# Two chained MLPs after attention on one core: the last layer in seven block products from a DRAM scratch, Softplus as one instruction, phases by an integer

## The chip, the core and the metric

The kernel runs on one core of a Trainium2 chip. TensorE (PE) multiplies matrices, VectorE (DVE) and ScalarE (ACT) do the work by element, GpSimd (POOL) next to nothing, SyncE (SP) issues the DMAs. The metric is the device time of one execution in microseconds; three runs of the kernel before had a median of 847.79 (846.71 to 847.88).

## The reference

```python
# attention: 4 x 8 heads, 576 tokens, 64 wide: a band of 7 neighbours, and softmax over 144 pooled tokens
out_up    = np.repeat(sm_attn(q_d, k_d, v_d), 4, axis=2)
out_local = softmax(where(|i - j| < 4, q k^T / 8, -1e9)) @ v
x = (out_up + out_local)  ->  2304 x 512
# first MLP: 512 -> 2048 -> 512
h = x @ w_in;  g = np.maximum(h, 0.0) + np.log1p(np.exp(-np.abs(h)));  x = g @ w_out
# second MLP: 512 -> 2048 -> 512, weights of its own
h = x @ w_in;  g = h * np.cos(h);  return (g @ w_out).astype(np.float32)
```

The MLP weights come as 64-bit floats, which the kernel decodes to 32 bits with shifts and ors.

## The kernel before

Each large product is three fp16 matmuls: operands are scaled and cut into a high and a low half, and hi x hi, hi x lo and lo x hi are added up in PSUM. Tokens are worked in five tiles (0 to 3 of 512 rows, 4 of 256; `TILES`), the 2048 hidden units in 16 units of 128.

Attention and the first MLP overlap. In the first MLP, for every tile and unit, `unit_in` (L1341) multiplies 12 matmuls into PSUM tile `h`; ScalarE makes |h|, relu(h), exp(-|h|) and ln(1 + ...) of it (L1438, L1442, L1446, L1450), VectorE adds them with the scale (L491, called by `mix`), `gh` (L501 on ScalarE or L503 on VectorE) makes the high half and `gl` (L483) the low half; the output layer follows at L1522. Meanwhile the second MLP's weights are loaded and decoded in `Weight.decode` (L636 a ScalarE rebase, L480 and L644 VectorE shift and or, L666 a bound for the scale), `split` makes their halves, and they stay in SBUF, in the space of the first MLP's weights as it comes free.

The input layer of the second MLP is already in seven block products instead of eight (`pair_in`): a pair of units is 7 products of 6 matmuls of 256 columns (L1376), with 14 fp16 blocks of 128 x 256 of weights (halves of 7 combinations), one kept product (`keep`, L1404) and four block sums on VectorE (L483, tile `hs`). Tile 4 takes the plain form (`last_in`). Then `rest_in` works out the activation: ScalarE h/2pi + 1/4 (`turns`, L1463), VectorE rounds it by adding and taking off a large constant (L1468) and subtracts (`rest`, L483 to `ta`), ScalarE takes the sine (L1474), VectorE multiplies with h (`G`, L1478), then `gh` and `gl`. The output layer `l4` (L1572) is the plain product, 512 columns a matmul, with both weight halves in SBUF; its scaled results (L495, L497) are stored by 18 DMAs. Before each tile, `y_in` prepares the input (sums, halves, a maximum for the scale).

The order of the instructions is not that of the code. Every operation is handed to a planner with its engines, a cost, its reads and writes and the buffers it claims; the planner orders each engine's queue by costs and due times, shifted by a table of numbers by operation (`MOVES`), and the order is then fixed. An engine takes its queue in order.

Of the kernel before, what the change touches and what calls it, by code (L numbers as in the profile page):

```python
# [15 lines left out]
I32 = mybir.dt.int32  # L16
I64 = mybir.dt.int64
# [9 lines left out]
NB = NF // 2  # L27
# [6 lines left out]
TWOPI = float(np.float32(2.0 * np.pi))  # L34
INV2PI = float(np.float32(1.0 / (2.0 * np.pi)))
T23 = float(1 << 23)
BELOW = 12
# [20 lines left out]
NST2, NTC, NOS, NHS, NPU = 2, 2, 4, 2, 4  # L58
# [6 lines left out]
W2STEP = 3  # L65
# [97 lines left out]
class Op:  # L163
    def __init__(self, n, cost, fn, claim, name):
        self.n, self.cost, self.fn, self.claim, self.name = n, cost, fn, claim, name
        self.succ, self.wait, self.values = set(), 0, set()
        self.hook, self.key = None, ""
# [238 lines left out]
def build(tc, qk, vw, vd, mask, w1i, w1o, w2i, w2o, out):  # L406
# [3 lines left out]
    with ExitStack() as ctx:  # L410
# [1143 lines left out]
        def l4(t, f):  # L1554
# [3 lines left out]
            if apart:  # L1558
                nd = 2
# [375 lines left out]
```

## Time and profile before

| | |
|---|---|
| median of 3 runs | 847.79 us |
| profiled execution, span | 847.6 us |
| TensorE busy | 834.0 us (98%) |
| VectorE busy | 719.1 us (85%) |
| ScalarE busy | 533.6 us (63%) |
| moved by DMA | 59.57 MB |

An execution is one span from the first instruction to the last. Busy time of an engine is the time in which at least one of its instructions was in work, so an instruction that starts before the one ahead of it has ended counts only for what it adds. Because of this overlap, the distance between two starts in a packed stretch is shorter than the duration listed. The chain of waits follows the work that ended last back to the start. Line numbers are those of the kernel before.

### The profile page before, as it was taken

Reading aid. Unit: us, or ns where it says so; the run is one execution under the profiler, and the core shown is the slowest. Engines: PE = TensorE matmul, PEld = TensorE weight load, DVE = VectorE, ACT = ScalarE, POOL = GpSimd, SP = SyncE. Lnnn points to the kernel's source line nnn. Section 1 sums busy time; section 2 is a strip of 40 time slices with the busy share of each in tenths; the row PEclk is TensorE's granted clock in tenths of the full one; section 3 lists DMA queues with packets and bytes.
Section 4 is the critical chain, followed back from the end, with each engine's and each line's share of the span. In section 5 each row is a group of like instructions: output and inputs, shape, how many; then the busy total and the mean of one; then the engine's idle time right before and its main releaser. Section 6 shows DMA issues by size and latency. Waiting matters only on the chain.

```text
span 847.6 us, 15741 instructions
## 1 busy us (share of the span) xinstructions
PE 834.0 (98%) x6325; PEld 493.8 (58%) x6325; DVE 719.1 (85%) x1482; ACT 533.6 (63%) x964; POOL 1.8 (0%) x9
## 2 busy tenths in 40 slices
PE   8988999999999999999999999999999999999998
PEld 4634545455545555444467886676666565676664
DVE  7989999997767858999968999998779679889763
ACT  5478996686635747699977876556444335555441
POOL 0000000000000000000000000000000000000000
PEclk9999999999999999999999999999999999999999
DMA  9876441112110300342023200000000100100010
GB/s 321 281 277 240 162 173 41 51 33 64 61 45 1 117 1 2 120 178 100 1 99 107 94 2 1 1 1 29 23 1 1 51 1 1 51 1 2 2 50 25
DMA packets 14361, 59.57 MB, mean 70 GB/s; under 512 B 1681, under 2 KB 1809, under 8 KB 10193
## 3 DMA queue, kind: packets, MB, share of 16 engines
q1 hardware_dynamic: 14288, 58.58, 19.9%
q8 instruction: 49, 0.80, 0.4%
q14 instruction: 24, 0.19, 0.1%
HBM read 53.85 MB, written 4.72 MB: 69 GB/s over the span
## 4 chain that ended last, share of the span: by engine, by line
PE 89%; ACT 5%; DVE 3%; DMA 2%; issue 0%; POOL 0%; POOLq 0%; ACTq 0%; SPq 0%
PE any L1572 22%; PE h L1376 20%; PE any L1522 19%; PE h L1341 19%; PE any L1314 1%; PE any L1097 1%; PE any L1850 1%; DMA stg<-w1o 1%; PE any L817 1%; PE any L972 1%; PE h L1277 1%; DMA stg<-w1i 1%; ACT w1i_t L636 1%; ACT w1i_t L495 0%; DVE w1i_t L644 0%; ACT ed L937 0%
## 5 line engine op out<-in xcount | busy, mean ns | idle before, releaser
L1572 PE MATMUL any<-w1i_t,g 128*128 128x512 f16 x864 | 197.8, 379 | 0.5 <-DVE w1o_t L497 0.5
L1341 PE MATMUL h<-xt,w1i_t 128*128 128x512 f16 (+1 forms) x888 | 179.5, 356 | 0.1
L1376 PEld LDWEIGHTS <-w2i_t 128*128 128x128 f16 x1536 | 150.2, 98 | 31.6 <-issue 0.3
L1522 PE MATMUL any<-g,w1o_t 128*128 128x512 f16 (+1 forms) x792 | 157.2, 353 | 0.0
L1572 PEld LDWEIGHTS <-g 128*128 128x128 f16 x864 | 84.5, 98 | 88.4 <-issue 1.1
L1341 PEld LDWEIGHTS <-w1i_t 128*128 128x128 f16 x888 | 86.1, 98 | 83.0 <-issue 2.6
L1522 PEld LDWEIGHTS <-w1o_t 128*128 128x128 f16 x888 | 85.7, 98 | 79.9 <-issue 1.4
L483 DVE TENSOR_TENSOR g<-td,g 128x512 f16<-128x512 f32 (+1 forms) x146 | 92.0, 630 | 8.9 <-ACT g L501 6.0
L1376 PE MATMUL h<-xt,w2i_t 128*128 128x256 f16 x720 | 94.3, 273 | 0.1
L1474 ACT ACTIVATE tc<-ta 128x512 f32<-128x512 f32 (+1 forms) x80 | 46.8, 585 | 66.7 <-DVE ta L483 64.6
L1376 PE MATMUL h<-w1o_t,w2i_t 128*128 128x256 f16 x624 | 78.9, 273 | 0.0
L501 ACT ACTIVATE g<-td 128x512 f16<-128x512 f32 (+1 forms) x81 | 48.4, 598 | 38.8 <-DVE td L1478 28.1
L1463 ACT ACTIVATE ta<-hs,quarter,i 128x512 f32<-128x512 f32 x64 | 51.5, 808 | 30.2 <-DVE hs L483 29.6
L1438 ACT ACTIVATE ta<-h,i 128x512 f32<-128x512 f32 (+1 forms) x74 | 47.1, 637 | 25.7 <-PE h L1341 21.4
L1478 DVE SCALAR_TENSOR_TENSOR td<-hs,r,tc 128x512 f32<-128x512 f32 x64 | 48.0, 750 | 13.7 <-ACT tc L1474 12.5
L483 DVE TENSOR_TENSOR hs<-h,hs 128x512 f32<-128x512 f32 (+1 forms) x96 | 57.2, 598 | 2.4 <-PE h L1376 1.6
L483 DVE TENSOR_TENSOR ta<-ta,tb 128x512 f32<-128x512 f32 (+1 forms) x80 | 50.9, 636 | 1.4
L1442 ACT ACTIVATE tb<-h,r 128x512 f32<-128x512 f32 (+1 forms) x74 | 47.1, 636 | 5.9 <-PE h L1341 4.0
L1450 ACT ACTIVATE ta<-ta,one 128x512 f32<-128x512 f32 (+1 forms) x74 | 49.8, 675 | 1.4
L491 DVE SCALAR_TENSOR_TENSOR td<-ta,sg,tb 128x512 f32<-128x512 f32 (+1 forms) x64 | 43.6, 682 | 7.8 <-ACT ta L1450 6.8
L1468 DVE TENSOR_SCALAR tb<-ta 128x512 f32<-128x512 f32 (+1 forms) x80 | 31.8, 398 | 17.1 <-ACT ta L1463 16.3
L1446 ACT ACTIVATE ta<-ta 128x512 f32<-128x512 f32 (+1 forms) x74 | 43.1, 585 | 0.3
(198 smaller groups left out, 1045.1 us busy)
## 6 DMA issues: line engine op xcount, KB each, us to landing
qk<-qk SPq DMA_DIRECT2D x16, 589.0 KB, 5.9
stg<-w1i SPq DMA_DIRECT2D x8, 1024.0 KB, 6.0
stg<-w1o SPq DMA_DIRECT2D x8, 1024.0 KB, 5.0
stg<-w2i SPq DMA_DIRECT2D x8, 1024.0 KB, 4.9
stg<-w2o SPq DMA_DIRECT2D x8, 1024.0 KB, 4.7
vw<-vw SPq DMA_DIRECT2D x16, 320.0 KB, 5.5
out<-w1o_t SPq DMA_DIRECT2D x18, 256.0 KB, 2.0
vd<-vd SPq DMA_DIRECT2D x8, 288.0 KB
```

Of the source, the lines that this page charges most:

```text
L483: eng[e].tensor_tensor(out=out, in0=in0, in1=in1, op=op)
L501: nc.scalar.activation(out=out, in_=in_, func=AF.Copy)
L1341: nc.tensor.matmul(h.t[:, 0:n], l, r, start=(i == 0), stop=(i == 11))
L1376: nc.tensor.matmul(h.t[:, a : a + 256], l, r, start=(i == 0), stop=(i == n - 1))
L1438: act(n, 1, True), lambda: nc.scalar.activation(out=a(), in_=h.t[:, 0:n], func=AF.Abs, scale=col(o.i1, f)),
L1442: act(n, 1, True), lambda: nc.scalar.activation(out=b(), in_=h.t[:, 0:n], func=AF.Relu, scale=col(o.r1, f)),
L1450: act(n, 1), lambda: nc.scalar.activation(out=a(), in_=a(), func=AF.Ln, bias=one),
L1463: act(n, 2, psum), lambda: nc.scalar.activation(out=a(), in_=h.t[:, a0 : a0 + n], func=AF.Identity, scale=col(o.i2, f), bias=quarter), [h, ...
L1474: act(n), lambda: nc.scalar.activation(out=r(), in_=a(), func=AF.Sin, scale=TWOPI),
L1478: dve(n, False, 1), lambda: nc.vector.scalar_tensor_tensor(out=td.t[:, 0:n], in0=h.t[:, a0 : a0 + n], scalar=col(o.r1, f), in1=r(), op0=AL ...
L1522: nc.tensor.matmul(a.t[:, i, 0:n], l, r, start=(first and j == 0), stop=(last and j == 2))
L1572: nc.tensor.matmul(a.t[:, i], l, r, start=(f == 0 and j == 0), stop=(f == NF - 1 and j == 2))
```

## The change

1. **Output layer of the second MLP** in seven block products: 256-column matmuls, 336 a tile (168 in tile 4) in place of 192 (96) of 512 columns. Its left operands are seven blocks of g for a pair of units, four of them sums made on VectorE (`S`), and all seven get a high and a low half. Seven VectorE instructions a tile join the products to the result, and the results are stored in pieces of 256 columns.
2. **DRAM scratch.** The decoded and split matrices of the second MLP are written to DRAM (`scr_in`, `scr_out`) and streamed back for every tile: for a pair of units 917 KB into one of two buffers (`RI`), for an output product two halves of 524 KB into two of four (`RO`). Decoding has a second ScalarE pass (`top`) and one VectorE instruction fewer. All these loads are in SP's queue.
3. **Softplus.** In tiles 1 to 4 of the first MLP a single ScalarE instruction takes the place of |h|, relu, exp, ln and VectorE's sum; attention pairs from the eighth on take their exponentials as Softplus of a value lowered by 20. Functions of different tables now follow each other on ScalarE: 48 table loads in the program instead of 2.
4. **Phases.** `turns` writes an integer; one VectorE instruction multiplies h again and takes that integer off; the rounding instruction goes, and the quarter turn is given to the sine.
5. Tile 2 of the second MLP's input layer takes the plain form (512 columns). Tile 0's input layer runs among tile 4 of the first MLP. From tile 2 on, ScalarE makes a sum of magnitudes (`xsum`) where VectorE made a maximum. The table `MOVES` is new throughout.

```diff
-NST2, NTC, NOS, NHS, NPU = 2, 2, 4, 2, 4
+NST2, NDEC, NRI, NRO, NTC, NHS, NPU, NGF = 2, 4, 2, 4, 3, 2, 3, 2
+ONES, FROM, LONG = range(0, 10, 2), (4, 0), (2, 4)
 MOVES = {
-    "L1 0 0": -32.5, "L1 0 10 exp#1": 38.5, "L1 0 10 gl#1": 66, "L1 0 10 mm#1": 57, "L1 0 11 abs#1": 73,
+    "L1 0 0": -800, "L1 0 1": 102, "L1 0 1 mm#1": -108, "L1 0 10 relu#1": 41.5, "L1 0 11": 13, "L1 0 12 mm#1": -24.5,
...
+        def block_in(t, b):
+            w = RI.new()
+            P.add(
+                dma(917), lambda: nc.sync.dma_start(w.t, scr_in[b]), [("scr", "w2i", b), "place3"], [w], [w], f"L3 {t} {2 * b} load"
+            )
+            return w
...
+        def turn_in(t, f, h, keys, g, psum, a0=0, hold=()):
...
+                    out=bits(a()), in_=x(), func=AF.Identity, scale=col(o.i2, f), bias=quarter
...
+                    out=a(), in0=x(), scalar=col(o.i2, f), in1=bits(a()), op0=ALU.mult, op1=ALU.subtract
...
+                act(n, 1), lambda: nc.scalar.activation(out=r(), in_=a(), func=AF.Sin, scale=TWOPI, bias=halfpi),
...
+        def parts_in(t, b, g):
...
+            for o, a, c, op in ((1, 7, 4, ALU.add), (2, 1, 0, ALU.subtract), (3, 0, 7, ALU.subtract), (5, 6, 2, ALU.subtract)):
+                P.add(dve(n), lambda o=o, a=a, c=c, op=op: two("dve", at(o), at(a), at(c), op), [], [g], name=nm + "S")
...
+            for v, a, m in ((u[0][0], 0, 1), (u[1][0], 1, 2), (u[3][0], 3, 2), (u[5][0], 5, 2)):
...
+                P.add(dve(n * m), lambda x=x, hi=hi, lo=lo: two("dve", lo(), x(), hi(), ALU.subtract), [g], [v], [], nm + "gl")
...
+            if t:
+                v = (TA, TB)[f % 2].new()
+                x = lambda: v.t[:, 0:n]
+                P.add(
+                    act(n, 1, True), lambda: nc.scalar.activation(out=x(), in_=h.t[:, 0:n], func=AF.Softplus, scale=col(o.i1, f)),
+                    [h, *sc], [v], [v], nm + "soft", table="sp",
+                )
...
+            then = [
+                (0, 0, 0, lambda: p.update(p1=take(0))), (1, 2, 5, lambda: p.update(u2=join(1, p["p1"], OS_.new()))),
+                (2, 1, 4, lambda: None), (3, 3, 1, seventh),
+                (0, 4, 6, lambda: out_rows(join(0, p["u3"], p["u3"]), 1, 0)),
+                (1, 5, 3, lambda: out_rows(join(1, p["u4"], p["u4"]), 0, 1)),
+                (2, 6, 2, lambda: out_rows(join(2, p["p1"], p["p1"]), 0, 0)),
+            ]
+            for j, (k, s, pos, fn) in enumerate(then):
+                ws = []
+                for h in range(2):
+                    w = RO.new()
+                    ws.append(w)
+                    P.add(
+                        dma(524), lambda w=w, pos=pos, h=h: nc.sync.dma_start(w.t, scr_out[:, pos, 4 * h : 4 * h + 4]),
+                        [("scr", "w2o", b) for b in range(NB)] + ["place3"], [w], [w], f"L4 {t} {j} load",
+                    )
+                for c in range(m):
+                    for b in range(NB):
...
+                            for x, (l, r) in enumerate(((gh, wh), (gh, wl), (gl, wh))):
+                                nc.tensor.matmul(
+                                    a.t[:, z, 256 * c : 256 * c + 256], l, r, start=(b == 0 and x == 0),
+                                    stop=(b == NB - 1 and x == 2),
+                                )
...
+                def store():
+                    if self.name == "w2i":
+                        nc.sync.dma_start(scr_in[b], both())
+                    else:
+                        for h in range(2):
+                            nc.sync.dma_start(scr_out[:, :, b, h], both()[:, h].rearrange("p (k e) -> p k e", k=7))
```

How the order of VectorE's queue reads in the second MLP, while pairs of tile 0 are in work, before (`hs` are the joined sums of h, `ta` and `tb` the turns and their rounded form, `tc` the sine, `td` the product, `g` halves, `xt` the next tile's input):

```order
L1468 TENSOR_SCALAR tb_97<-ta_94 128x512
L491 SCALAR_TENSOR_TENSOR xt_81<-xt_81,sx_199,xs_99 128x512
L483 TENSOR_TENSOR ta_94<-ta_94,tb_97 128x512
L483 TENSOR_TENSOR hs_4944<-h_757,pu_4947 128x512
L1250 COPY xt_81<-xs_99 128x512
L1478 SCALAR_TENSOR_TENSOR td_98<-hs_4943,r_0_169,tc_4941 128x512
L1234 TENSOR_REDUCE xm_212<-xt_82 128x1
L483 TENSOR_TENSOR hs_4943<-h_756,hs_4943 128x256
L483 TENSOR_TENSOR g_102<-td_98,g_102 128x512
L491 SCALAR_TENSOR_TENSOR xt_81<-xt_81,sx_199,xs_99 128x512
L1468 TENSOR_SCALAR tb_96<-ta_95 128x512
```

And after, with pairs of tile 1 in work (`gf` holds the eight blocks of g of a pair; the low halves go into the space of the first MLP's weights, `w1i_t` and `w1o_t`):

```order
L1509 SCALAR_TENSOR_TENSOR ta_98<-hs_4429,i_1_180,ta_98 128x512
L513 TENSOR_TENSOR hs_4430<-h_3135,hs_4430 128x512
L513 TENSOR_TENSOR gf_4434<-gf_4434 128x256
L513 TENSOR_TENSOR hs_4430<-h_3134,hs_4430 128x256
L513 TENSOR_TENSOR gf_4434<-gf_4434 128x256
L1509 SCALAR_TENSOR_TENSOR ta_97<-hs_4430,i_1_180,ta_97 128x512
L533 CAST w1o_t<-gf_4434 128x512
L1518 SCALAR_TENSOR_TENSOR gf_4435<-hs_4429,r_1_183,tc_4428 128x2x256
L513 TENSOR_TENSOR w1i_t<-gf_4434,w1i_t 128x256
L513 TENSOR_TENSOR w1o_t<-gf_4434,w1o_t 128x512 x2
L1509 SCALAR_TENSOR_TENSOR ta_98<-hs_4430,i_1_180,ta_98 128x512
L513 TENSOR_TENSOR w1i_t<-gf_4434,w1i_t 128x512
```

The rounding (L1468) is gone; the remainder (L1509) has become a three-operand instruction. Sums within `gf` stand between the input layer's sums, and four low halves a pair stand where two stood, three of them as wide as before.

ScalarE's queue in the first MLP, where the second MLP's weights are decoded, before (`w2i_t` is a weight block, `h` a unit's product):

```order
L495 ACTIVATE w2i_t<-w2i_t,s_w2i 128x1792
L1450 ACTIVATE ta_95<-ta_95,one 128x512
L495 ACTIVATE tx_3405<-tx_3405,sx_175 128x512
L1438 ACTIVATE ta_94<-h_757,i_3_201 128x512
L501 ACTIVATE g_103<-td_98 128x512
L1446 ACTIVATE ta_94<-ta_94 128x512
L1442 ACTIVATE tb_96<-h_756,r_3_205 128x512
L1450 ACTIVATE ta_94<-ta_94,one 128x512
L501 ACTIVATE g_105<-td_98 128x512
```

And after (`stg` is a block as loaded, `dec` the decoded one, L1869 the rebase, L1874 the added pass, L1887 the bound, L1553 Softplus):

```order
L525 ACTIVATE g_110<-tb_99,sg_194 128x512
L1869 ACT_TABLE_LOAD
L1869 ACTIVATE dec_3168<-stg_3166 128x1024
L1874 ACTIVATE stg_3166<-stg_3166,nearhalf 128x1024
L1869 ACTIVATE dec_3169<-stg_3167 128x1024
L1553 ACT_TABLE_LOAD
L1553 ACTIVATE ta_97<-h_781,i_2_191 128x512
L1887 ACT_TABLE_LOAD
L1887 ACTIVATE stg_3166,bd_w2i<-dec_3168 128x1024
L1874 ACTIVATE stg_3167<-stg_3167,nearhalf 128x1024
L1887 ACTIVATE stg_3167,bd_w2i<-dec_3169 128x1024
L1553 ACT_TABLE_LOAD
```

Four functions a unit have become one, and each change between Softplus and the decode's functions has a table load ahead of it.

## Rows read from the trace of the kernel before

**Rows 1.** The page's busy times: us, share of the span, instructions

```profile
PE 834.0 (98%) x6325; PEld 493.8 (58%) x6325; DVE 719.1 (85%) x1482; ACT 533.6 (63%) x964; POOL 1.8 (0%) x9
```

**Rows 2.** The page's chain of waits, by engine and by line

```profile
PE 89%; ACT 5%; DVE 3%; DMA 2%; issue 0%; POOL 0%; POOLq 0%; ACTq 0%; SPq 0%
PE any L1572 22%; PE h L1376 20%; PE any L1522 19%; PE h L1341 19%; PE any L1314 1%; PE any L1097 1%; PE any L1850 1%; DMA stg<-w1o 1%; PE any L817 1%; PE any L972 1%; PE h L1277 1%; DMA stg<-w1i 1%; ACT w1i_t L636 1%; ACT w1i_t L495 0%; DVE w1i_t L644 0%; ACT ed L937 0%
```

**Rows 3.** Busy times by stretch (us; instructions; granted clock; DMA share; GB/s)

```profile
150.00:300.00 150.00, 150.00 (x1317) 77.59 (x1315) 123.38 (x280) 98.62 (x197) 0.00 (x0) 1.00 0.15 50
300.00:430.00 130.00, 129.99 (x791) 64.27 (x789) 117.50 (x249) 101.96 (x164) 0.00 (x0) 1.00 0.19 65
...
600.00:700.00 100.00, 99.73 (x651) 63.42 (x649) 75.34 (x128) 39.72 (x63) 0.00 (x0) 1.00 0.03 11
...
520.00:560.00 40.00, 40.00 (x270) 26.11 (x267) 40.00 (x84) 22.97 (x37) 0.00 (x0) 1.00 0.00 1
```

**Rows 4.** Pieces of the chain: start us, length us, what

```profile
488.28 9.84 PE h L1376 x90
...
829.45 14.26 PE any L1572 x66
...
843.73 0.69 ACT w1o_t L495
```

**Rows 5.** Groups of TensorE by line and form: busy us, mean ns

```profile
L1572 PE MATMUL any<-w1i_t,g 128*128 128x512 f16 x864 | 197.8, 379 | 0.5 <-DVE w1o_t L497 0.5
...
L1376 PEld LDWEIGHTS <-w2i_t 128*128 128x128 f16 x1536 | 150.2, 98 | 31.6 <-issue 0.3
```

**Rows 6.** Timeline of VectorE in the second MLP: start us, length us

```profile
531.96 0.75 DVE L1478 SCALAR_TENSOR_TENSOR td<-hs,r,tc 128x512 f32<-128x512 f32 x1
532.62 0.42 DVE L1234 TENSOR_REDUCE xm<-xt 128x1 bf16<-128x256 f32 x1
532.95 0.42 DVE L483 TENSOR_TENSOR hs<-h,hs 128x256 f32<-128x256 f32 x1
533.28 0.42 DVE L1468 TENSOR_SCALAR tb<-ta 128x512 f32<-128x512 f32 x1
533.61 0.69 DVE L483 TENSOR_TENSOR g<-td,g 128x512 f16<-128x512 f32 x1
534.21 0.69 DVE L483 TENSOR_TENSOR ta<-ta,tb 128x512 f32<-128x512 f32 x1
```

**Rows 7.** Groups of VectorE by line and form: busy us, mean ns

```profile
L1478 DVE SCALAR_TENSOR_TENSOR td<-hs,r,tc 128x512 f32<-128x512 f32 x64 | 48.0, 750 | 13.7 <-ACT tc L1474 12.5
...
L644 DVE SCALAR_TENSOR_TENSOR w2i_t<-stg,w2i_t 128x1024 int32<-128x1024 int32 x8 | 9.8, 1223 | 0.0
```

**Rows 8.** Groups of ScalarE by line and form: busy us, mean ns

```profile
L1450 ACT ACTIVATE ta<-ta,one 128x512 f32<-128x512 f32 x58 | 41.7, 721 | 1.0
...
L1438 ACT ACTIVATE ta<-h,i 128x512 f32<-128x512 f32 x58 | 39.7, 684 | 25.1 <-PE h L1341 21.4 <-DVE td L491 2.7 <-DVE am L1217 0.7
L1442 ACT ACTIVATE tb<-h,r 128x512 f32<-128x512 f32 x58 | 39.6, 683 | 4.0 <-PE h L1341 4.0
L1446 ACT ACTIVATE ta<-ta 128x512 f32<-128x512 f32 x58 | 36.5, 631 | 0.1
...
L636 ACT ACTIVATE w2i_t<-stg 128x1024 f32<-128x1024 f32 x8 | 9.2, 1149 | 1.2 <-DMA stg<-w2i 1.2
```

**Rows 9.** Timeline of ScalarE around its second table load

```profile
495.16 0.81 ACT L1463 ACTIVATE ta<-hs,quarter,i 128x512 f32<-128x512 f32 x1 [0.57 <-DVE hs L483]
495.99 1.28 ACT L1474 ACT_TABLE_LOAD   x1
```

**Rows 10.** The page's GB/s by slice, and DMA issues (KB each, us to landing)

```profile
GB/s 321 281 277 240 162 173 41 51 33 64 61 45 1 117 1 2 120 178 100 1 99 107 94 2 1 1 1 29 23 1 1 51 1 1 51 1 2 2 50 25
...
stg<-w2i SPq DMA_DIRECT2D x8, 1024.0 KB, 4.9
...
out<-w1o_t SPq DMA_DIRECT2D x18, 256.0 KB, 2.0
```

More of the change, by code (lines that the diff above doesn't have):

```diff
@@ L180, in __init__, with add @@
         self.ops, self.wrote, self.read, self.time = [], {}, {}, {}
-    def add(self, cost, fn, reads=(), writes=(), claim=(), name="", after=()):
-        op = Op(len(self.ops), cost, fn, claim, name)
+    def add(self, cost, fn, reads=(), writes=(), claim=(), name="", after=(), table=""):
+        op = Op(len(self.ops), cost, fn, claim, name, table)
         pre = set(after)
@@ L329, in order @@
                     end = now + op.cost[e]
+                    if e == "act" and loaded not in SETS[op.table]:
+                        end, loaded = end + LOAD, SETS[op.table][0]
                     free[e] = end
@@ L726, in build, with aop @@
         stages = {}
-        def aop(cost, fn, reads=(), writes=(), claim=(), name=""):
+        def aop(cost, fn, reads=(), writes=(), claim=(), name="", table=""):
             stage = name.split()[-1]
-            op = P.add(cost, fn, reads, writes, claim, name, stages.get(stage, ()) if claim else ())
+            op = P.add(cost, fn, reads, writes, claim, name, stages.get(stage, ()) if claim else (), table)
             if claim:
@@ L937, in B2 @@
                     nc.scalar.activation(
-                        out=row(t), in_=src, func=AF.Exp, scale=float(2.0**-7),
+                        out=row(t), in_=src, func=power, scale=float(2.0**-7),
                         bias=nd.t[:, t : t + 1], accum_out=r.t[:, 2 * NG + t : 2 * NG + t + 1],
@@ L1237, in max_x, with sum_x, total @@
             )
+        def sum_x(t, c):
+            v = TC_.new()
+            def total():
+                with nc.allow_low_precision(reason="a bound, for the choice of a scale"):
+                    nc.scalar.activation(
+                        out=v.t[:, 0 : TILES[t][1]], in_=xt[t][:, c, :], func=AF.Abs, accum_out=col(T[t].xm, c)
+                    )
+            P.add(act(TILES[t][1], 1), total, [xkey(t, c), "place3"], [("xm", t, c), v], [v], name="xsum", table="pr")
         def split_x(t, c):
@@ new lines, in turn_in @@
+            P.add(
+                act(n, 1), lambda: nc.scalar.activation(out=r(), in_=a(), func=AF.Sin, scale=TWOPI, bias=halfpi),
+                [ta, "place3"], [tr], [tr], nm + "sin", table="tr",
+            )
+            P.add(
+                dve(n, False, 1), lambda: nc.vector.scalar_tensor_tensor(
+                    out=at(), in0=two_of(x()), scalar=col(o.r1, f), in1=two_of(r()), op0=ALU.mult, op1=ALU.mult
+                ), [*keys, tr, *sc], [g], [g, *hold], nm + "G",
+            )
@@ new lines, in join, with seventh @@
+            def join(k, x, o):
+                P.add(
+                    dve(256 * m, False, 1), lambda: nc.vector.scalar_tensor_tensor(
+                        out=o.t[:, 0 : 256 * m], in0=view(k), scalar=T[t].ik, in1=x.t[:, 0 : 256 * m],
+                        op0=ALU.mult, op1=ALU.add,
+                    ), [(t, k), x, ("sc", t)], [o], [o, acc[k][0]], "osb",
+                )
+                return o
+            p = {}
+            def seventh():
+                p["u4"] = p["u2"]
+                p["u3"] = join(3, p["u2"], OS_.new())
+                join(2, p["u2"], p["u2"])
+                out_rows(join(2, p["u3"], OS_.new()), 1, 1)
@@ L1700, in tx_part @@
+        W2I, W2O = Second("w2i", w2i), Second("w2o", w2o)
+        txs = [TX.new() for _ in range(5)]
         def tx_part(t, u, n=1):
-            return (txs[t].t if t else tx0[0])[:, 512 * u : 512 * (u + n)]
+            return txs[t].t[:, 512 * u : 512 * (u + n)]
         def tx_float(t, k):
@@ L1741, in y_in @@
             for c in range(NC_):
-                if c < 2 and t < 4:
+                if c < 2 and t not in LONG:
                     split_half(t, c)
@@ L1813, in build @@
+        drain(0)
         for p in sorted(pos):
             assert p < at, (p, at)
[L1815 to L1834 removed]
@@ L1835, in build @@
-        drain(0)
+        mms = {W: [o for o in P.ops if o.name[:3] == k and "pe" in o.cost] for W, k in ((W1I, "L1 "), (W1O, "L2 "))}
+        for W, ops in mms.items():
+            for u in range(NF + 1):
+                bs = [b for b in range(NB) if u in (W.hunit(b), W.funit(b))]
+                names = [f"{t} {f}" for t in range(5) for f in range(NF) if f // 2 in bs]
+                free_slots([o for o in ops if " ".join(o.name.split()[1:3]) in names], W, u)
+        P.add({"pool": 0.01}, lambda: None, [], [], [], "dead", after=[o for m in ends_of for o in m]).hook = (
+            lambda: OS_.free.extend(range(NGS))
+        )
@@ L1837, in build @@
+        pair_ops = None
+        for t in range(4):
+            work = l4(t)
+            for b in range(NB):
+                if b == YIN // 2 and t < 3:
+                    y_in(t + 2)
+                (last_in if t + 1 in LONG else pair_in)(t + 1, b)
+                for _ in range(14):
+                    next(work, None)
+            for _ in work:
+                pass
+        for _ in l4(4):
+            pass
         zero = const.tile([128, 128], F16, name="zero")
```

501 lines of the change are left out of this document (302 added, 199 removed), and 130 rows, old and new, of the table MOVES.

## The prediction

> **What bounds the kernel now.** I read the busy shares first [rows 1]. TensorE works 834.0 of 847.6 us. VectorE has 719.1, ScalarE 533.6. The reader should take from it that the time is the sum of the matmuls, and that VectorE is the only engine near enough to take over. The chain of waits says the same [rows 2]: 89% of it is TensorE, in four lines with about a fifth of the span each (the input and output layers of both MLPs, L1341, L1522, L1376, L1572). The granted clock is 1.00 in every stretch of the windows [rows 3], the 2.4 GHz level, so nothing is to be had there. The windows also show where the other engines stand: in the middle of the first MLP (150 to 430 us) VectorE is busy 241 of 280 us and ScalarE 201; in the second MLP (600 to 700 us) VectorE has 75 of 100 and ScalarE 40. TensorE is full in all of them.
>
> **Working time and ends.** The page times an execution of 847.6 us; the median of three runs is 847.8. The difference, 0.2 us, is kept as it is and lost in rounding. After the last matmul group (829.45 + 14.26 = 843.71 us) come one scaling of 0.69 us and the store, 3.9 us together [rows 4]. The changed kernel ends in the same way (a join of half the size, then a store), so this stays.
>
> **TensorE, the output layer of the second MLP.** The chain gives the spacing of matmuls in an unbroken run [rows 4]: 66 of 512 columns in 14.26 us, 0.216 us each; 90 of 256 columns in 9.84 us, 0.109 us each. So a narrow matmul with its own weight load costs half a wide one. Before, L1572 has 864 wide ones [rows 5]: 186.7 us. After, seven block products instead of eight give 4 x 336 + 168 = 1512 narrow ones: 165.3 us. Term: -21.4 us.
>
> The Trainium skill, "TensorE: Matmul & The Clock Gate", section "Back-to-back issue gap", speaks against such a change: it gives a sustained 131 ns for 512 columns and 81 ns for 128, so that narrow matmuls would not get cheaper in proportion. By interpolation between those two (an estimate, about 97 ns at 256) the layer would go from 113 to 147 us and the kernel would lose 34. The trace does not agree (216 and 109 ns), and it measures both widths in this very kernel, so I give that rule no chance.
>
> **TensorE, the input layer.** Before: 1536 narrow matmuls [rows 5], 167.9 us. After, tile 2 uses the plain form with two weight blocks per unit: 192 wide ones for its 336 narrow ones, so 1200 narrow and 192 wide, 131.2 + 41.5 = 172.7 us. Term: +4.8 us. The first MLP and attention keep their matmuls. The eight added filler matmuls are put where TensorE would idle; I count 0. Sum for TensorE alone: 847.6 - 21.4 + 4.8 = 831.0 us.
>
> **VectorE in the second MLP.** This is where the gain can be lost, because the new layer takes matmuls away and adds vector work. Prices are distances between starts of instructions that run back to back [rows 6]: 0.66 us for a three-operand one of 512 columns (531.96 to 532.62), 0.33 for a two-tensor one of 256 (532.95 to 533.28), 0.33 for the rounding form of 512, 0.60 for a two-tensor one of 512. For one pair of units, before: block sums of the input layer 3 x 0.60 + 0.33 = 2.13, rounding 2 x 0.33 = 0.66, remainder 2 x 0.60 = 1.20, the product h cos h 2 x 0.66 = 1.32, low halves 2 x 0.60 = 1.20; 6.5 us. After: 2.13, no rounding, remainder as a three-operand instruction 1.32, product 1.32, four block sums of h cos h 4 x 0.33 = 1.32, low halves of seven blocks 3 x 0.60 + 0.33 = 2.13; 8.2 us. The remainder now reads an integer operand. No such instruction of 512 columns is in the trace; the nearest are an integer one of 1024 columns at 1223 ns and the float one of 512 at 750 ns [rows 7]. Half the first is 0.61 us, so I take 0.66, with 0.60 and 0.75 as ends (-4 to +6 us of VectorE work over 64 whole and 16 half instructions). Seven output joins a tile are 7 x 0.66 / 8 = 0.6 us a pair, and the preparation of a later tile (sums and low halves at 0.60 and 0.66, a dozen a tile) about 1.0. So 9.8 us of VectorE a pair.
>
> TensorE has 42 + 42 narrow matmuls a pair: 9.2 us (before 42 narrow and 24 wide, 9.8). The engine that was idle a quarter of the time becomes the longer one by 0.6 us a pair, in 24 pairs (tiles 0, 1 and 3): 14 us at most, if nothing absorbs it. What absorbs some: tile 0 runs beside the last tile of the first MLP, which brings TensorE other work; tile 2 in its plain form needs no block sums (VectorE 6.1 + 1.6, TensorE 42 x 0.109 + 24 x 0.216 = 9.8 a pair); tile 4 is half as wide. From the first of these products to the end I count, with the same prices, about 328 us of VectorE against 362 of TensorE, so it is no bound as a whole, only in places. I take 6 us of TensorE idle, a little under half of 14; ends 0 and 20 (14 and the integer operand's 6).
>
> **ScalarE.** From tile 1 on, four functions of the first MLP (684, 683, 631 and 721 ns [rows 8]) and a VectorE sum become one Softplus. The trace has no Softplus; nearest are those four, and I take the first, which also reads the matmul's result with a pointer scale. That saves 3 x 0.6 us on 64 units, some of them 256 wide: about 93 us with the shorter conversion partly lost again. Added: 46 table loads. There are two loads in the trace; the one at 495.99 us takes 1.28 and starts 0.02 us after the instruction before it has ended (495.16 + 0.81) [rows 9]. 46 x 1.28 = 59. A second pass of 1024 columns on 16 weight blocks, by the rebase's 1149 ns [rows 8] less overlap, 17. Sums over tiles in place of VectorE's maximum, 7. High halves of seven blocks instead of four, about 20. Net +10 us on an engine that has 314 idle. The place to look at is the decode of the second MLP's weights: in the new order ScalarE has between the first decode and the first cosine 37 loads (47 us) and 101 us of other work, 148 in all, while TensorE has 816 matmuls of the first MLP (34 units), 161 us. This fits with 13 us over: I take 0; ends -1 (VectorE freed of 64 sums there, with TensorE already full) and +10 (ScalarE's waits for loads and for VectorE's joins inside that stretch, which hold the Softplus behind them).
>
> The Trainium skill, "ScalarE: Activation LUTs", section "What ACT_TABLE_LOAD costs", gives 1283 ns for the load, as the row has it, and about 1380 ns more of draining for every switch. The row shows no such gap ahead of the load; with it ScalarE would have 51 us more in that stretch.
>
> **DRAM scratch.** The decoded matrices go out once and come back for every tile: 40 loads of 917 KB and 70 of 524 KB, all on SP's queue, where a load that waits for its buffer holds the next ones. The nearest rows are loads of 1024 KB in 4.9 us and stores of 256 KB in 2.0 [rows 10]. A pair lasts 9.2 us and its 917 KB take less than 5 into the other of two buffers: hidden. A product takes 48 x 0.109 = 5.2 us and needs 1.05 MB, at most 5 us, into the pair of buffers that the product before the last has left: hidden, barely. Rate over the stage: 73 MB in 362 us, 203 GB/s; the trace has moved 321 in its first slice. In the last tile a product takes only 2.6 us, which asks for 400 GB/s; at 321 it is 3.3 us, and five of seven are not preloaded: 5 x 0.65 = 3 at most, I take 1. The gate between the last store and the first load back is covered by the last tile of the first MLP, 0; without that cover a store and a load, some 10 us.
>
> Sum: 831.0 + 6 + 1 + 0 = 838 us.
>
> **Rivals.**
> (a) TensorE keeps full, as it does now in every window: 831. For it: the order of instructions can work ahead on output products, 42 matmuls a pair that wait for nothing of that pair. Against: VectorE was already busy 40 of 40 us in one place of the lighter version (520 to 560 us [rows 3]), and now has a quarter more a pair.
> (b) Late streaming: each of 35 output products waits 0.4 us for its block, since 5 us of load stand against 5.2 of work and a store of results lies between: 14 us, 845.
> (c) ScalarE becomes the bound of the decode stretch. It takes its instructions in order, so a rebase that waits for its weights holds the Softplus behind it. If each of the 16 blocks waits a quarter of its 4.9 us load, 20 us, ScalarE needs 168 us against 161: 7 us on top of the forecast, 845.
> (d) VectorE becomes the bound in tiles 0, 1 and 3. The steps of a pair go back and forth between both engines (turns, remainder, sine, product, sums, high, low), and with two buffers for sums and products it cannot stay packed: with busy times in place of distances (0.69 and 0.75 for 0.60 and 0.66) a pair is 11.4 us, not 9.8. At 1.0 us a pair over TensorE, 24 pairs: 831 + 24 = 855. It makes the kernel slower from 0.7 us a pair on (16.8 / 24). For it: VectorE has nowhere been packed for long in [rows 3]; against: most of its idle time there was not needed.
> (e) Each table switch costs a second stall as long as the load: 47 us in the stretch, less 13 spare, on top of the forecast: 838 + 34 = 872. The draining that the section named above states would be such a stall; the row at 495.99 us speaks against it.
>
> **Chances.** Forecast (832.5 to 843) 45%, (a) 22%, (b) 10%, (c) 9%, (d) 11%, (e) 3%. A measurement of this kernel can tell about 0.2% from no change, so same is 846.1 to 849.5. Faster: 45 + 22 + 5 of (b) + 5 of (c) = 77%; same: 3 of (b), 2 of (c), 3 of (d) = 8%; slower: 2 + 2 + 8 + 3 = 15%. The range must leave out no more than 2 in 10: 828 (a with one unit of luck in the fillers and the ends) to 855; the forecast's own range is 832.5 to 843.
>
> **What would show it.** Right: the new output line with 1512 matmuls at 0.109 us; VectorE busy over 9 tenths through the second MLP, TensorE idle 5 to 10 us there, released by VectorE's low halves or block sums; ScalarE under 9 tenths in the decode stretch with loads of 1.28 us. The forecast is wrong if TensorE waits on DMA into the streamed buffers (b), on Softplus with ScalarE full (c), or idles more than 17 us in all on VectorE (d); or if a 256-column matmul with its weight load takes over 0.12 us, which would cost 16 us alone.

## The result: slower by 1.3%, and the profile after

The changed kernel takes 859.73 us (858.18 to 859.96, four runs) against 847.84 for the kernel before: ratio 1.0129, 95% interval 1.0105 to 1.0152. A later comparison gave 1.0103 (1.0079 to 1.0127), so steps counted from the first are uncertain by some 2 us. The forecast was 838, the range ended at 855. Line numbers from here on are those of each run's own kernel: L1722, L1729 and L1734 are the matmul of the output layer, L1430 and L1442 that of the input layer.

The page first: busy times, then the chain of waits by engine.

```profile
PE 822.7 (96%) x6837; PEld 543.3 (63%) x6837; DVE 734.8 (86%) x1570; ACT 543.5 (63%) x924; POOL 1.8 (0%) x9
...
PE 75%; DMA 11%; ACT 9%; DVE 4%; issue 1%; SPq 0%; POOL 0%; POOLq 0%; ACTq 0%
```

TensorE is busy 11.3 us less than before [rows 1], and the span is 10.5 us longer (858.1 for 847.6). So TensorE stands idle some 22 us more. In the chain DMA has come up from 2% to 11% [rows 2]. The windows of the changed kernel show where (columns as in [rows 3]):

```profile
0.00:150.00 150.00, 137.51 (x1318) 72.68 (x1319) 136.16 (x266) 114.52 (x224) 1.77 (x9) 0.99 0.62 208
150.00:300.00 150.00, 150.00 (x1522) 80.77 (x1521) 114.25 (x282) 61.74 (x139) 0.00 (x0) 1.00 0.14 42
300.00:430.00 130.00, 126.87 (x600) 57.73 (x598) 108.81 (x207) 115.79 (x124) 0.00 (x0) 1.00 0.55 194
430.00:520.00 90.00, 88.14 (x703) 68.14 (x701) 85.69 (x181) 77.57 (x124) 0.00 (x0) 1.00 0.52 176
520.00:600.00 80.00, 76.29 (x697) 67.67 (x696) 77.71 (x161) 53.10 (x94) 0.00 (x0) 1.00 0.49 164
600.00:700.00 100.00, 97.41 (x702) 68.37 (x700) 96.86 (x208) 57.01 (x97) 0.00 (x0) 1.00 0.60 200
700.00:800.00 100.00, 97.99 (x892) 86.79 (x890) 91.81 (x203) 53.16 (x99) 0.00 (x0) 1.00 0.70 228
800.00:859.00 59.00, 48.46 (x418) 41.13 (x416) 23.51 (x69) 10.66 (x26) 0.00 (x0) 0.96 0.69 223
```

Each line gives the stretch and then the busy time of TensorE, its weight loads, VectorE, ScalarE and GpSimd; stretch less TensorE's busy time is its idle time. The same subtraction on the windows of four kernels gives this table; "no reloads" and "both" are runs told below, and the last row ends with the last matmul (843.7, 854.8, 836.5 and 840.1 us).

| stretch (us) | before | after | no reloads | both |
|---|---|---|---|---|
| 0 to 150 | 8.5 | 12.5 | 11.1 | 11.9 |
| 300 to 430 | 0.0 | 3.1 | 3.1 | 3.1 |
| 430 to 520 | 0.6 | 1.9 | 0.7 | 0.9 |
| 520 to 800 | 0.3 | 8.3 | 2.3 | 2.3 |
| 800 to the end | 0.3 | 6.3 | 0.8 | 1.7 |
| sum | 9.7 | 32.1 | 18.0 | 19.9 |

Not every difference in the first row is one of the kernels. The first reload starts at 466 us, so a run without reloads does the same work up to there; the 15 profiled executions with the changed order idle 10.9 to 14.4 us in the first 150, and the two with the order of before 8.5 and 10.1.

What TensorE waited for in the changed kernel (us in all, times, the longest):

```profile
PE any L1722 <- DMA ro<-scr_out: 7.3, 8, 1.7
PE h L1430 <- DMA ri<-scr_in: 5.4, 6, 2.1
PE h L1322 <- ACT ed L971: 2.5, 1, 2.5
PE any L1722 <- DVE g L1681: 2.4, 3, 1.3
...
PE h L551 <- ACT stg L1887: 1.8, 1, 1.8
...
PE any L1623 <- DVE g L521: 1.3, 1, 1.3
```

The two largest are the streamed blocks: `ro` (output layer) and `ri` (input layer), 12.7 us. The chain in the last tile shows how such a wait comes about (start us, length us, what):

```profile
820.76 5.90 DMA ro<-scr_out
826.66 0.04 issue
826.70 5.74 PE any L1722 x51
832.46 5.36 DMA ro<-scr_out
837.82 0.04 issue
837.86 6.67 PE any L1722 x45
...
846.26 5.33 DMA ro<-scr_out
```

A load starts when matmuls have let go of a buffer, lands 5.3 to 5.9 us later, and only then do the matmuls go on that need it. Input blocks come late in the same way (two pieces of the chain, then TensorE's timeline with its wait in brackets):

```profile
565.32 0.67 PE h L1430 x6
566.00 7.28 DMA ri<-scr_in
...
573.33 1.48 PE L1430 MATMUL h<-tx,ri 128*128 128x256 f16 x12 [2.06 <-DMA ri<-scr_in]
```

TensorE had 5.3 us of other work in between, to 571.27, and the load took 7.28. All twelve loads on the chain after 465 us start within 0.03 us of the end of the matmuls before them, so none of these stood ready behind another load in the queue; they took 5.3 to 7.4 us to land. The issues of the two kinds (KB each, median us to landing) say that landings of about 5 us are the normal case:

```profile
ri<-scr_in SPq DMA_DIRECT2D x40, 896.0 KB, 4.6
ro<-scr_out SPq DMA_DIRECT2D x70, 512.0 KB, 4.9
```

The smaller load does not land sooner than the larger.

### The profile page after: what moved, and what is told of

Read it like the earlier page. It is cut to its first block, busy times and chain, and to the rows that moved or that the text cites. A ratio compares the mean times of both kernels' runs of the same rounds, so it can differ in the third digit from the quotient of the medians.

```text
span 858.1 us, 16959 instructions
## 1 busy us (share of the span) xinstructions
PE 822.7 (96%) x6837; PEld 543.3 (63%) x6837; DVE 734.8 (86%) x1570; ACT 543.5 (63%) x924; POOL 1.8 (0%) x9
## 4 chain that ended last, share of the span: by engine, by line
PE 75%; DMA 11%; ACT 9%; DVE 4%; issue 1%; SPq 0%; POOL 0%; POOLq 0%; ACTq 0%
PE any L1623 19%; PE h L1430 17%; PE any L1722 16%; PE h L1386 15%; DMA ro<-scr_out 4%; DMA ri<-scr_in 4%; DMA qk<-qk 1%; PE any L1131 1%; DMA stg<-w1i 1%; ACT w1i_t L696 1%; PE any L847 1%; PE any L1006 1%; ACT ta L1560 1%; ACT tb L1564 1%; ACT ta L1572 1%
## 5 line engine op out<-in xcount | busy, mean ns | idle before, releaser
L1430 PEld LDWEIGHTS <-ri 128*128 128x128 f16 x1392 | 135.6, 98 | 41.6 <-DMA ri<-scr_in 7.4
L1386 PEld LDWEIGHTS <-w1i_t 128*128 128x128 f16 x888 | 86.1, 98 | 84.5 <-issue 4.0
L1623 PEld LDWEIGHTS <-w1o_t 128*128 128x128 f16 x888 | 85.8, 98 | 80.2 <-issue 2.6
L1722 PE MATMUL any<-ro,w1o_t 128*128 128x256 f16 x744 | 107.8, 275 | 6.6 <-DMA ro<-scr_out 5.9
L1430 PE MATMUL h<-xt,ri 128*128 128x256 f16 (+1 forms) x720 | 109.5, 294 | 3.8 <-DMA ri<-scr_in 3.1
L1722 PE MATMUL any<-ro,w1i_t 128*128 128x256 f16 x768 | 108.1, 273 | 3.8 <-DVE g L1681 1.9
L1430 PE MATMUL h<-tx,ri 128*128 128x256 f16 (+1 forms) x672 | 91.4, 280 | 2.3 <-DMA ri<-scr_in 2.3
L1722 PEld LDWEIGHTS <-w1i_t 128*128 128x128 f16 x768 | 75.1, 98 | 15.6 <-issue 3.9
L1722 PEld LDWEIGHTS <-w1o_t 128*128 128x128 f16 x744 | 73.1, 99 | 18.1 <-issue 6.4
L1514 ACT ACTIVATE tc<-ta,halfpi 128x512 f32<-128x512 f32 (+1 forms) x80 | 53.4, 675 | 33.2 <-DVE ta L1509 23.3
L513 DVE TENSOR_TENSOR gf<-gf 128x256 f32<-128x256 f32 (+1 forms) x160 | 58.6, 391 | 0.1
L513 DVE TENSOR_TENSOR w1i_t<-gf,w1i_t 128x512 f16<-128x512 f32 (+2 forms) x91 | 46.6, 526 | 1.7 <-ACT w1i_t L531 1.4
L1553 ACT ACTIVATE ta<-h,i 128x512 f32<-128x512 f32 (+1 forms) x32 | 20.1, 632 | 25.8 <-PE h L1386 25.6
```

Of the source, the lines that this page charges most:

```text
L513: eng[e].tensor_tensor(out=out, in0=in0, in1=in1, op=op)
L1386: nc.tensor.matmul(h.t[:, 0:n], l, r, start=(i == 0), stop=(i == 11))
L1430: nc.tensor.matmul(h.t[:, a : a + m], l, r, start=(i == 0), stop=(i == n - 1))
L1514: act(n, 1), lambda: nc.scalar.activation(out=r(), in_=a(), func=AF.Sin, scale=TWOPI, bias=halfpi),
L1553: act(n, 1, True), lambda: nc.scalar.activation(out=x(), in_=h.t[:, 0:n], func=AF.Softplus, scale=col(o.i1, f)),
L1623: nc.tensor.matmul(a.t[:, i, 0:n], l, r, start=(first and j == 0), stop=(last and j == 2))
```

## The experiments

**Is it the streaming? Reloads left out.** Each reload is made only for the first use of its buffer. Later matmuls work with old blocks, which is the part of the computation that these three runs leave out; the order on TensorE, VectorE and ScalarE is the same, instruction by instruction.

```diff
-                dma(524), lambda w=w, pos=pos, h=h: nc.sync.dma_start(w.t, scr_out[:, pos, 4 * h : 4 * h + 4]),
+                dma(524), lambda w=w, pos=pos, h=h: once(w, lambda: nc.sync.dma_start(w.t, scr_out[:, pos, 4 * h : 4 * h + 4])),
...
-                dma(917), lambda: nc.sync.dma_start(w.t, scr_in[b]),
+                dma(917), lambda: once(w, lambda: nc.sync.dma_start(w.t, scr_in[b])),
```

> Only the first load of each of the four output-layer buffers is made, the other 66 loads of 512 KB are left out; every instruction of TensorE, VectorE and ScalarE stays, in the same order. Theory A (streaming: TensorE waits for buffers whose reload lands 5 us after they come free): the waits on the output-layer blocks go, about 7 us of direct waits and what follows them, some 13 us, the last tile losing most; 859.7 to about 846. Theory B (VectorE is the bound of the second MLP, loads only seem late): VectorE waits take their place, 856 to 860.

> Only the first load of each of the two input-layer buffers is made, the other 38 loads of 896 KB are left out; the rest in the same order. Theory A: the 5.4 us of direct waits on these blocks go, and the output blocks land a little sooner because less is in flight; about 852. Theory B: 857 to 860.

> Both kinds of reload are left out, the rest in the same order. Theory A: all of the 20 us by which starts of matmuls in the second MLP stand further apart than packed go, less a few that VectorE then holds; about 840, and faster than before. Theory B: VectorE waits replace them, 855 or more.

Measured against the kernel before in the same comparison: without output-block reloads 0.9960 (0.9948 to 0.9973), without input-block reloads 1.0015 (1.0002 to 1.0029), without both 0.9931 (0.9908 to 0.9953). From 1.0129 these are steps of 1.7, 1.1 and 2.0%: 14, 10 and 17 us. Theory A holds, B falls: no VectorE wait takes the place (the wait for the output joins is 2.6 us, and 2.4 in the changed kernel). The two steps do not add up to the third. The traces point to each kind of load delaying the other: with input blocks alone TensorE's wait for them falls as well,

```profile
PE h L1430 <- DMA ri<-scr_in: 1.9, 2, 1.2
```

from 5.4 to 1.9 us (run without output-block reloads; a second profile of the changed kernel has 3.1), and with output blocks alone these land in 4.0 us where they took 4.9, and are waited for 6.1 us where it was 7.3.

**Are table loads the price? Relu in place of Softplus.** The activation itself is left out by this; 4 table loads remain of 48.

```diff
-func=AF.Softplus, scale=col(o.i1, f)
+func=AF.Relu, scale=col(o.i1, f)
```

> Softplus of the first MLP's tiles 1 to 4 is replaced by Relu, which needs no table of its own, so that table loads go from 48 to about 6; the activation is left out, the order stays. Theory A: the table loads hide except in the decode stretch, where TensorE stood 3.5 us (waits on a scale and on low halves); 3 to 4 us less, about 856. Theory C (table switches are what makes the kernel slow): 10 us or more less, 850 or below.

1.0118 (1.0073 to 1.0162), no difference that can be told from the changed kernel. ScalarE is busy 487 us for 543, and TensorE's idle time in the decode stretch (300 to 430 us) is 2.9 us for 3.1; its waits of 1.8 and 1.3 us there are still 1.5 and 1.4. So theory C falls, and the 3 to 4 us that A expected back did not come either: the 3.1 us are not the tables'. The 1.8 us are a wait for ScalarE's bound of a weight block (L1887), which stands behind the rebase, the added pass and a VectorE step of that block. The 1.3 us are VectorE's: in its queue two low halves of weight blocks stand ahead of a unit's low half that the matmuls wait for:

```profile
375.11 0.48 DVE L527 TENSOR_SCALAR g<-ta,sg 128x512 f16<-128x512 f32 x1
375.50 4.08 DVE L521 SCALAR_TENSOR_TENSOR dec<-dec,s_w2i 128x1792 f16<-128x1792 f32 x2
379.49 0.75 DVE L521 SCALAR_TENSOR_TENSOR g<-ta,sg,g 128x512 f16<-128x512 f32 x1
```

**Rate, queue or ring?** Three explanations for late loads: bytes (S), the one queue (Q), or too few buffers for a landing of 5 us (L).

```diff
 # ro_half
-nc.sync.dma_start(w.t, scr_out[:, pos, 4 * h : 4 * h + 4])
+nc.sync.dma_start(w.t[:, 0:2], scr_out[:, pos, 4 * h : 4 * h + 2])
-wh, wl = w.t[:, b % 4, 1], w.t[:, b % 4, 0]
+wh, wl = w.t[:, b % 2, 1], w.t[:, b % 2, 0]
 # outq
+for c in range(m):
+    nc.gpsimd.dma_start(dst[:, c], o.t[:, 256 * c : 256 * c + 256])
 # roq
-nc.sync.dma_start(w.t, scr_out[:, pos, 4 * h : 4 * h + 4])
+nc.gpsimd.dma_start(w.t, scr_out[:, pos, 4 * h : 4 * h + 4])
 # deep: slots that a load of a tile may take; the one used longest ago is taken
+may = base + [5 + k for k in range(2 * int(op.name.split()[1]))]
+i = min(may, key=lambda i: old.get(i, -1))
```

> Each of the 70 output-block loads brings the first half of its bytes (256 KB, 2 KB a partition), and the matmuls use these twice; number, order and waits of the loads stay. Theory S (bytes: the landing of 4.9 us is 512 KB sharing the rate with other loads): landing about 2.5 to 3 us, nearly all of the 14 us go that leaving out these loads gave back, ratio to the kernel before about 1.000. Theory L (a fixed time from issue to use in a ring of four buffers): landing still about 4 us, a third of the gain at most, about 1.008.

> The 20 stores of results are issued from GpSimd's queue instead of SP's, in two pieces each, so that a store that waits for a join no longer holds the loads behind it; all else in the same order. Theory Q (the single queue is what makes the loads late; SP waited 7.3 us for joins in the last 59 us): 4 to 6 us less, ratio about 1.007. Theories S and L: under 2 us less, 1.011 or more.

> The 70 output-block loads are issued from GpSimd's queue instead of SP's, so that neither they nor the input-block loads wait for each other's buffers; all else in the same order. Theory Q: half of the 17 us that all reloads cost go, ratio about 1.003. Theories S and L: about 1.010, since a buffer still comes free at the same time; slower if a load from that queue takes longer to land than 4.9 us.

> The output-block loads get more buffers: a fifth one, and two more in the input space of every tile that is done (13 in tile 4 instead of 4), taken in turn; the order on every engine stays, nothing is left out. Theory L: TensorE no longer waits for output blocks from tile 1 on, the last tile loses 2 us instead of 9; about 10 us less, ratio about 1.001. Theory S: bytes are the same, and the last tile asks for 400 GB/s; 3 to 4 us less, about 1.009. Theory Q: the queue still holds the loads back, under 3 us less.

Half the bytes: 0.9979 (0.9958 to 1.0000), 13 us back, nearly as much as without these loads. The ratio is the one that S expected; L's 1.008 is missed. The landing lies between the two, and did not halve with the bytes:

```profile
ro<-scr_out SPq DMA_DIRECT2D x70, 256.0 KB, 3.1
```

3.1 us for 4.9: it seems that a part of it does not depend on size. The Trainium skill, "DMA: Bandwidth & Descriptors", section "Anatomy of one DMA — SWDGE (gpsimd) path", fits a time of 2.0 us plus bytes at 436 KB a microsecond for a DMA on GpSimd's path; an estimate by it is 2.6 and 3.2 us for the two sizes. The trace agrees in that half the bytes take more than half the time; its landings, from SP's queue, are longer (3.1 and 4.9 us), with other loads on the way at the same time.

Stores from GpSimd's queue: 1.0180 (1.0146 to 1.0214), no gain, so Q falls in the form tried, stores that hold loads. Output blocks from GpSimd's queue: 1.1026 (1.0990 to 1.1061), 10% slower. That was far outside what any theory expected. The timeline of GpSimd in the last tile shows loads one at a time, 4.0 to 4.1 us apart:

```profile
897.69 0.53 POOL L1709 DMA_DIRECT2D ro<-scr_out  x1 [3.57 <-issue]
901.82 0.54 POOL L1709 DMA_DIRECT2D ro<-scr_out  x1 [3.59 <-issue]
905.84 0.54 POOL L1709 DMA_DIRECT2D ro<-scr_out  x1 [3.49 <-issue]
```

Each landed in 3.8 us (median), sooner than from SP's queue, but the next did not start before. What holds it in GpSimd was not looked into; the run says nothing on Q beyond that, and a second queue that keeps several loads on the way was not tried. Against Q stand the twelve loads told above, which started as their buffers came free.

The deep ring, nothing left out: 1.0007 (0.9985 to 1.0028), 10 us back. Its loads are *slower* than before, and TensorE hardly waits for them (deep ring; issues, then waits):

```profile
ro<-scr_out SPq DMA_DIRECT2D x41, 512.0 KB, 5.7
xt<-scr_out SPq DMA_DIRECT2D x29, 512.0 KB, 7.6
```

```profile
PE h L1442 <- DMA ri<-scr_in: 1.8, 3, 0.8
...
PE any L1734 <- DMA ro<-scr_out: 0.2, 1, 0.2
```

So the same bytes are in time if they are asked for earlier. S had expected 1.009 here and L 1.001, and this decides for L against a plain bound by rate. Nor was the rate used up: in the last tile, the changed kernel and then the run with both rings deep, told below, moved (last number, GB/s)

```profile
820.00:830.00 10.00, 8.29 (x77) 7.28 (x76) 8.34 (x28) 4.26 (x11) 0.00 (x0) 1.00 0.71 228
...
820.00:830.00 10.00, 10.00 (x93) 8.94 (x92) 2.65 (x7) 0.47 (x1) 0.00 (x0) 1.00 1.03 413
```

Bytes count all the same, through the landing: halving them shortens the time from a free buffer to its next contents.

**Step by step.** Two runs meant to vary the ring gave blocks their buffers in a fixed turn, by which, it seems, some were overwritten before their last use; part of the products then used wrong blocks, and loads waited for other users than intended (TensorE's wait for input blocks rose to 12.7 us in the first).

```diff
+for j, v in enumerate(vs):
+    v.i = j % n
```

> Five output-block buffers instead of four, taken in turn, the order on every engine as it is; nothing is left out. Theory L (the ring is too short for a landing of 5 us): in the last tile a half block is used for 1.3 us, so five buffers cover 4 x 1.3 = 5.2 us instead of 3.9; the last tile loses 3 to 4 us instead of 9, ratio about 1.006. Theory S (rate of the loads in the last tile): under 2 us less, 1.011.

> As the run with up to 13 output-block buffers, but the input space of tile 0 becomes a third input-block buffer from the middle of tile 1 on (the output blocks then have 5 buffers and two more for each of tiles 1 to 3 that is done); nothing is left out. Theory L: the 1.8 us of waits on input blocks go too, the sum comes to within 3 us of the run without reloads; ratio 0.997, faster than both kernels. If loads only push each other back: 1.001, as before.

They took 1.0241 (1.0211 to 1.0271) and 0.9983 (0.9965 to 1.0002), and decide nothing. The next two choose a buffer only when its last user stands earlier in the order:

```diff
+can = [i for i in range(len(until)) if until[i] < k]
+v.i = min(can, key=lambda i: until[i])
+until[v.i] = lastuse[v]
```

> Five output-block buffers instead of four, each taken once its last user is past; the order on every engine as it is, nothing left out. Theory L (ring too short for a landing of 5 us): the last tile loses 4 to 5 us instead of 9, the tiles before 1 to 2 us less; 6 us less than the changed kernel, ratio to before about 1.006. Theory S (rate): 2 us less at most.

> Five output-block buffers and two more in the input space of each of tiles 1 to 3 when it is done; the input space of tile 0 is a third input-block buffer when it is done. Nothing left out. Theory L: nearly all waits on loads go; within 3 us of the run without reloads, ratio about 0.997. If the input blocks are not what is left of the loss: 1.001, as with the deep ring for output blocks alone.

> The changed kernel as it is, for comparison on the same chip: ratio 1.011 to 1.015.

Changed kernel 1.0103 (1.0079 to 1.0127), one buffer more 1.0024 (1.0008 to 1.0041), both rings deep 0.9963 (0.9949 to 0.9977). The waits follow (the changed kernel again, one buffer more, then both rings deep):

```profile
PE any L1722 <- DMA ro<-scr_out: 7.2, 10, 1.3
...
PE h L1430 <- DMA ri<-scr_in: 3.1, 5, 1.9
```

```profile
PE h L1442 <- DMA ri<-scr_in: 1.8, 4, 1.0
...
PE any L1734 <- DMA ro<-scr_out: 1.7, 4, 0.9
```

```profile
PE any L1734 <- DVE g L1693: 2.6, 4, 1.3
...
PE any L1734 <- DMA ro<-scr_out: 0.8, 1, 0.8
```

7.2 + 3.1 (7.3 + 5.4 in the first profile of the changed kernel), 1.7 + 1.8, 0.8 + 0 us of waits for loads. The last leaves nothing out, and it is faster than the kernel before by 0.37%, and than the changed one by 1.4% in the same comparison. Four buffers under the new choice were not run, so the fifth buffer and the choice are not told apart; the deep ring, with the old choice for the input blocks, has the same 1.8 us for these.

**Is VectorE the next bound?** Without reloads, and without the block sums of h cos h:

```diff
-P.add(dve(n), lambda o=o, a=a, c=c, op=op: two("dve", at(o), at(a), at(c), op), [], [g], name=nm + "S")
+P.add(dve(n), lambda: None, [], [g], name=nm + "S")
```

> Without reloads and without the four block sums that VectorE makes of h cos h for each pair (160 instructions, 52 us of VectorE); these blocks hold zeros. Theory A (VectorE's added work lies beside TensorE): 0 to 2 us less than without reloads alone, ratio 0.991 to 0.993. Theory B (VectorE is the next bound, hidden until now by the loads): 4 us or more less, 0.988 or below.

0.9916 (0.9900 to 0.9932) beside 0.9931 without reloads alone: no gain that can be told, though VectorE is busy 692.6 us for 733.3. Theory A holds.

**Softplus alone, in the kernel before.**

> The kernel before with one part of the change alone: Softplus in tiles 1 to 4 of the first MLP in place of four functions (VectorE's sum becomes a scaling); its order stays as planned for the four, and 54 table loads stand in it instead of 2. Theory A (TensorE is full in that stretch, ScalarE's work and table loads lie beside it): ratio 0.998 to 1.002. Theory C (table switches cost time): 52 more loads at 1.3 us, of which a part holds TensorE: 1.006 or more.

```diff
-# four ScalarE functions (abs, relu, exp, ln) and VectorE's scaled sum
+nc.scalar.activation(out=a(), in_=h.t[:, 0:n], func=AF.Softplus, scale=col(o.i1, f))
+nc.vector.tensor_scalar_mul(td.t[:, 0:n], a(), col(sg, f))
```

1.0204 (1.0179 to 1.0228): 17 us slower, although ScalarE is busy 34 us less (499.3 for 533.6). Here theory C was right and mine wrong. TensorE idles 10 us between 430 and 520 us, and 4 between 300 and 430. With these waits the clock that it is granted between 430 and 520 is 0.96 on average, between its two levels of 1.2 and 2.4 GHz (windows of this run, then what TensorE waited for there):

```profile
430.00:520.00 90.00, 79.97 (x598) 59.38 (x596) 62.46 (x133) 69.55 (x90) 0.00 (x0) 0.96 0.19 71
```

```profile
PE h L521 <- ACT ta L1439: 5.4, 2, 3.6
PE h L521 <- ACT stg L666: 3.6, 1, 3.6
```

L521 is the small matmul that spreads a maximum over the partitions for a weight block's scale; it waits until Softplus (L1439) has read the PSUM tile that it writes to, or for ScalarE's bound (L666). It stands in TensorE's queue at the place planned for a ScalarE without table loads, and the matmuls behind it wait too. Eleven pieces of this run's chain between 450 and 500 us are table loads, 13.8 us together. So table loads are not free as such. The changed kernel hides them, as Relu shows; that this is because its order was laid out around them is likely, but no run tries it.

## Why the prediction was wrong, point by point

**What bounds the kernel, and the matmuls: right.** (The granted clock that I read as 1.00 throughout was 0.99 in the first 150 and the last 48 us, which changes nothing.) Narrow matmuls run at 0.109 us in the new layer too (changed kernel, chain):

```profile
794.86 7.20 PE any L1722 x66
```

The terms -21.4 and +4.8 stand. TensorE's busy time falls by 11.3 us, not 16.6. The eight fillers, which I put at nothing, are worked (1.7 us at 0.216), and 4.1 us go when the reloads go (818.6 us busy for 822.7). An estimate of these: a matmul ahead of a wait is counted with its whole 0.27 us instead of 0.109, in 14 waits for loads 2.3 us; and the run of 45 matmuls in the chain above took 6.67 us where 45 x 0.109 is 4.9, 1.8 us. It stands behind waits of 0.7 and 1.5 us, in a stretch with a granted clock between its levels:

```profile
835.00:840.00 5.00, 3.30 (x20) 2.38 (x21) 0.48 (x1) 0.00 (x0) 0.00 (x0) 0.77 0.78 278
```

The second profile of the changed kernel has an average of 1.00 from 800 us on.

**DRAM scratch: the step that failed.** I wrote "A product takes 48 x 0.109 = 5.2 us and needs 1.05 MB, at most 5 us, into the pair of buffers that the product before the last has left: hidden, barely", "A pair lasts 9.2 us and its 917 KB take less than 5 into the other of two buffers: hidden", and for the last tile 3 us at most, of which I took 1. These compare rates. A rate tells whether a queue that is always full keeps up; this queue is not full, since each load waits for its buffer (SP stood 154.5 us for output-block buffers and 153.4 for input-block ones). The right comparison is the time from a buffer's release to the landing of its next contents, against the work that TensorE has meanwhile from the *other* buffers. The loads that were waited for landed in 5.3 to 7.4 us, not in less than 5. In the last tile a half block is used up in 12 x 0.109 = 1.3 us. The other three of four hold 3.9 us, so that loads come up to 2 us late. A pair of units lasts 9.2 us on average, but in the order as it is one input block had 5.3 us until it was needed again, and the load took 7.28. I had the landing, 4.9 us for 1024 KB [rows 10], and scaled it with the bytes; the 256 KB store in the same rows, 2.0 us where a quarter of 4.9 is 1.2, could have told me not to. Reloads, taken at 1 us, cost 17 by ratio. In the profiled executions the difference is 18.3 (858.1 to 839.8): 12.7 of idle in the second MLP (16.5 to 3.8 in the table) and the 4.1 of TensorE's busy time, 16.8 together; the other 1.4 lie in the first 150 us, where there are no reloads, and are a difference between two executions. The last tile alone has 5.5 of them (6.3 to 0.8), where I had 3 at most; its 400 GB/s, which I held against 321, were there (413).

Rival (b), late streaming, named the wait, and the sign that I gave for it, TensorE waiting on DMA into the streamed buffers, came. Its 14 us are near the 12.7 of idle by luck: it had 35 equal waits of 0.4 us for output blocks, and there are 8 for output and 6 for input blocks, up to 2.1 us each. It had 10%, and I counted it from the ideal 831 up, as if it came alone; on top of the forecast it would have been 852.

**VectorE: the direction right, the size too large, the place another.** I took 6 us of idle, with 20 as the far end, released by low halves or block sums. VectorE is indeed full (96.86 of 100 us between 600 and 700, and 99.22 in the run with both rings deep), with 0.66 us between starts as taken, the integer operand making no difference:

```profile
L1509 DVE SCALAR_TENSOR_TENSOR ta<-hs,i,ta 128x512 f32<-128x512 f32 x48 | 35.6, 746 | 0.6 <-ACT ta L1504 0.6
```

746 ns, as the float one has [rows 7]. But what TensorE waits for there is only the output joins (2.4 us), and 41 us less of VectorE's work gained nothing. It seems that working ahead on output products absorbs the rest, as rival (a) had it: in the chain they stand between the products of the pairs. Rival (d) falls.

**ScalarE: taken at 0, and the table loads cost nothing here.** Softplus takes 686 ns and the added pass 1230, as the neighbours said (684 and 1149). The table load takes 1.28 us, and in the trace no time is lost around it:

```profile
374.34 1.78 ACT L525 ACTIVATE dec<-dec,s_w2i 128x1792 f16<-128x1792 f32 x1
376.14 1.28 ACT L1869 ACT_TABLE_LOAD   x1
377.43 1.15 ACT L1869 ACTIVATE dec<-stg 128x1024 f32<-128x1024 f32 x1
```

It starts 0.02 us after the end of the instruction before, and the next starts 0.01 us after its own. The draining of 1.4 us that the Trainium skill ("ScalarE: Activation LUTs", "What ACT_TABLE_LOAD costs") adds is not there, and rival (e) falls with it. Rival (c) did not come either. What I missed are 3.1 us of the decode itself: 1.8 for the bound of a block, and 1.3 behind VectorE's two low halves (4.08 us), which stand ahead of a unit in that stretch.

**Left out altogether:** the first 150 us. I counted attention as unchanged. Its matmuls are, but its order is new and its exponentials are others; TensorE idles 4.0 us more there in the two profiles compared, with a ScalarE exponential (2.5 us) as the largest wait; over all executions it is 10.9 to 14.4 us for 8.5 and 10.1. Which edit does it was not tried.

Together: 831.0 + 1.7 (fillers) + 16.8 (reloads) + 4.0 (0 to 150 us) + 3.1 (decode) + 2.6 (what is left in the second MLP, joins above all) is 859.2. The end after the last matmul is 0.6 us shorter (3.3 for 3.9 [rows 4]), which gives 858.6; measured 858.1. Without the reloads it is 841.8 (the run without them has a median of 842.6), which is inside the forecast's own range, 832.5 to 843. That is in part luck: what I left out (1.7 + 4.0 + 3.1) stands against a VectorE term that was too large.

## What to carry to other kernels

A streamed operand is hidden when the other buffers of its ring hold more work than the time from releasing a buffer to landing its next contents; test that, stage by stage and for the order as it is, with a landing measured while other transfers are on the way (here 5.3 to 7.4 us where the medians were 4.6 and 4.9), and only then the rate. Look for the stage with the least work a byte (here the half-wide last tile), and for space that is dead by then: a fifth output-block buffer and dead input space for both rings, with the order unchanged, turned 1.0% slower into 0.4% faster. And when several things may be late at once, add them before giving the sum a single chance.

## What the runs showed that was not expected

A load of 512 KB landed in 4.9 us where 896 KB took 4.6, and in 5.7 to 7.6 us when more were on the way. The last tile moved 413 GB/s over 10 us once its loads were asked for early enough. Loads of 512 KB from GpSimd's queue came one every 4.0 us. Replacing four ScalarE functions by one made the kernel before 2.0% slower, through 52 table loads at places where the order had left no room.
